# Score matmuls of 64 rows in the two halves of the array, and 256-column accumulators

## The chip, the cores and the metric

The kernel runs on one core of a Trainium2 chip. The metric is device time in microseconds (us) of one execution. The names of the engines are those of the profile: PE multiplies matrices (PEld is its weight load), DVE and ACT work element by element, POOL scatters rows, SP issues most DMAs. A matmul is written as 128x512 when it streams 512 columns through the array; its weights are loaded by an instruction of its own ahead of it.

## The reference

```python
scores = (1 / S) * z @ z.T               # z: 8 x 3072 x 64
attn = maximum(scores, 0) ** 2
x = (u * (attn @ v)).reshape(B * S, D)    # u, v: 8 x 3072 x 256
e = argmax(x @ w_gate)                    # 8 experts, in token order, 768 rows each at most
out = gate * (relu(disp[e] @ w1[e]) @ w2[e])   # F = 1024; rows past the capacity stay 0
```

Float32 products are made of fp16 pieces: each operand is split into a high and a low part (`h`, `l`), and a product is hi*hi + hi*lo + lo*hi, added up in float32 in PSUM. The gate decides which expert a row goes to, so the low parts cannot be left out.

## The kernel before

**Attention** goes by blocks of 512 queries (`CC` = 4 chunks of 128), 14 of them, the last a half block of 2 chunks; later tokens find all experts full. Six blocks are a batch. A block has 12 pairs of key tiles (`NPAIR`; a tile is 128 keys). For a pair the scores of two tiles are made (`scores`, L757 to L816), ACT takes the ReLU out of PSUM (L780) and squares both tiles at once (L784), DVE splits the squares into fp16 parts `hl` (L788, L797), and PE multiplies these with the split values `v2` (L872, L874) into the block's accumulators `acc`. Scores are symmetric, so a block whose mirror was computed earlier reads its scores back from DRAM, transposed by the DMA (`keep` L809, `load` L750, tile `ld`). 106 pairs are computed, 84 of them 512 columns wide and 22 of them 256 wide; the rest is loaded, or comes from a block's own corner (`corner`).

`zz` holds the split z, transposed, on 128 partitions: in `zz[:, 0]` the high part stands in partitions 0 to 63 and the low part in 64 to 127, in `zz[:, 1]` the other way round. So a tile's scores are two matmuls of all 128 rows (L772): one gives hi*hi + lo*lo, the other hi*lo + lo*hi.

A chunk's product with a key tile is two matmuls: the high weights against high and low values side by side, 512 columns (L872), and the low weights against the high values, 256 columns (L874). The accumulator has 512 columns, and its two halves are added when the block ends (`drain`, L839 on ACT, L840 on DVE). After that `route` multiplies with u (L556), finds the row's maximum (L561), splits, transposes, makes the gate's logits (`lg`), the running count (`cum`), and scatters the rows to their experts.

**Experts**: per expert up to 768 rows, `hps` (L1012, three matmuls per product as above) and `yps` (L1033, L1034, built like the attention's product), then ACT and DVE scale and add the two halves (L1040, L1043) and POOL scatters.

PSUM has 8 banks: 2 for scores (`sc`, and `yps`), 4 for accumulators (`acc`, and `hps`), 2 for the small tiles (`m`: transposed z, logits, counts).

The order of the work is written by a planner inside the kernel: it runs the instructions of PE in program order and keeps a clock per engine from a table of costs (`op`); pieces of work on the other engines wait in chains, and `weave` emits those that are due by these clocks. `need` marks what PE waits for. Scores are emitted up to three pairs ahead, one tile in each half of a pair. Costs are 0.864 us for 1024 columns of scores (L774) and 0.325 us for a chunk's product with a tile (L876).

## Time and profile before

| | us |
|---|---|
| median of 3 runs (lowest, highest) | 807.35 (807.35, 810.51) |
| the profiled execution | 808.55 |
| its span, first to last instruction | 806.7 |

| engine | busy, share of the span |
|---|---|
| PE | 781.0 us, 97% |
| DVE | 536.7 us, 67% |
| ACT | 434.3 us, 54% |
| POOL | 130.2 us, 16% |

The profile is one execution. Matmuls overlap in it: a record runs from a matmul's start until its last result, and the next one starts long before that. What a matmul costs PE is therefore the distance from its start to the next start, not the length of its record.

### The profile page before, as it was taken

How to read it: one execution, taken by the hardware profiler on the slowest of the kernel's cores; microseconds unless marked ns; L12 is line 12 of the kernel's file. 1: busy time of each engine (PE TensorE's matmuls, PEld its weight loads, DVE VectorE, ACT ScalarE, POOL GpSimd, SP SyncE). 2: the span in 40 equal slices, each digit the busy share in tenths (PEclk: the TensorE clock that was granted, in tenths of full speed). 3: DMA queues.
4: the chain of work that ended last, by engine and by line, in shares of the span. 5: the costliest groups of instructions: out<-in, count | busy, mean ns of one | idle time of the engine just before them, and what ended most of it. 6: DMA issues, size and time to landing. Idle time of an engine off the chain costs nothing.

```text
span 806.7 us, 13434 instructions
## 1 busy us (share of the span) xinstructions
PE 781.0 (97%) x4964; PEld 460.7 (57%) x4964; DVE 536.7 (67%) x1186; ACT 434.3 (54%) x748; POOL 130.2 (16%) x123
## 2 busy tenths in 40 slices
PE   6999999999999999999999999999799999999996
PEld 2555555555655555555556655565566666666663
DVE  6886887863536889976454359888674675665741
ACT  5786746461405767763524148674564564554541
POOL 0000121110202010202112020203211313303202
PEclk8799999999999999999999999999999999999999
DMA  6399998969897996949597969972797847655001
GB/s 195 131 339 253 309 256 205 262 173 226 187 202 154 305 281 168 277 129 269 136 270 172 202 153 297 272 188 78 183 323 291 260 137 285 217 164 173 27 14 44
DMA packets 278736, 165.48 MB, mean 205 GB/s; under 512 B 218125, under 2 KB 244058, under 8 KB 278656
## 3 DMA queue, kind: packets, MB, share of 16 engines
q1 hardware_dynamic: 273760, 151.69, 71.3%
q0 software_dynamic: 4896, 12.79, 4.7%
q8 instruction: 42, 0.69, 0.4%
q14 instruction: 38, 0.31, 0.1%
HBM read 35.86 MB, written 77.75 MB: 141 GB/s over the span
## 4 chain that ended last, share of the span: by engine, by line
PE 87%; DMA 5%; DVE 3%; SPq 2%; ACT 2%; issue 1%; POOL 0%; POOLq 0%; ACTq 0%
PE acc L872 32%; PE acc L874 16%; PE hps L1012 14%; PE sc L772 10%; PE yps L1033 10%; PE yps L1034 5%; DMA ld<-kept 2%; DMA vraw<-in_v 1%; DMA fxt<-disp 1%; DMA zz<-zhl 1%; SPq L584 1%; DVE hh L998 1%; PE lg L591 0%; SPq L343 0%; ACT r L780 0%
## 5 line engine op out<-in xcount | busy, mean ns | idle before, releaser
L872 PE MATMUL acc<-v,hl 128*128 128x512 f16 x760 | 257.7, 381 | 2.9 <-DVE v L459 2.9
L874 PE MATMUL acc<-v,hl 128*128 128x256 f16 x760 | 208.2, 274 | 0.0
L780 ACT ACTIVATE r<-sc 128x512 f32<-128x512 f32 (+1 forms) x212 | 116.1, 551 | 140.3 <-PE sc L772 133.4
L872 PE MATMUL acc<-v,ld 128*128 128x512 f16 x488 | 162.4, 379 | 3.4 <-DMA ld<-kept 2.0
L874 PE MATMUL acc<-v,ld 128*128 128x256 f16 x488 | 133.0, 272 | 0.0
L1012 PE MATMUL hps<-fxt,wt 128*128 128x384 f16 (+2 forms) x816 | 127.2, 316 | 4.0 <-DVE hh L998 1.8
L1033 PE MATMUL yps<-wt,hh 128*128 128x512 f16 x384 | 125.5, 379 | 0.0
L872 PEld LDWEIGHTS <-hl 128*128 128x128 f16 x760 | 74.7, 98 | 88.4 <-issue 1.9
L772 PE MATMUL sc<-zz 128*128 128x512 f16 (+1 forms) x424 | 118.6, 364 | 3.6 <-DVE zz L395 2.3
L797 DVE TENSOR_TENSOR hl<-a,hl 128x1024 f16<-128x1024 f32 (+1 forms) x106 | 118.2, 1115 | 3.5
L84 POOL DMA_INDIRECT disp<-xr,slot x54 | 67.6, 1252 | 300.0 <-ACT a L784 147.7
L1012 PEld LDWEIGHTS <-wt 128*128 128x128 f16 x816 | 76.0, 98 | 54.1 <-issue 5.1
L1034 PE MATMUL yps<-wt,hh 128*128 128x256 f16 x384 | 104.7, 273 | 0.4 <-DVE hh L998 0.4
L788 DVE CAST hl<-a 128x1024 f16<-128x1024 f32 (+1 forms) x106 | 67.9, 640 | 54.9 <-ACT a L784 47.7
L784 ACT ACTIVATE a<-r 128x1024 f32<-128x1024 f32 (+1 forms) x106 | 102.6, 968 | 3.2
L998 DVE SCALAR_TENSOR_TENSOR hh<-hps,hh 128x384 f16<-128x384 f32 (+2 forms) x136 | 70.7, 530 | 39.2 <-ACT hh L997 38.8
L997 ACT ACTIVATE hh<-hps 128x384 f16<-128x384 f32 (+2 forms) x136 | 62.9, 471 | 49.6 <-PE hps L1012 49.0
L874 PEld LDWEIGHTS <-hl 128*128 128x128 f16 x760 | 74.7, 98 | 24.2 <-issue 2.2
L872 PEld LDWEIGHTS <-ld 128*128 128x128 f16 x488 | 47.7, 98 | 56.9 <-DMA ld<-kept 3.3
L84 POOL DMA_INDIRECT out<-ys,sid x48 | 55.2, 1150 | 124.3 <-DVE ys L1043 86.1
L1033 PEld LDWEIGHTS <-hh 128*128 128x128 f16 x384 | 37.5, 98 | 44.1
L1040 ACT ACTIVATE ys<-yps,sg 128x256 f32<-128x256 f32 x48 | 22.8, 475 | 74.1 <-PE yps L1034 67.1
(134 smaller groups left out, 685.1 us busy)
## 6 DMA issues: line engine op xcount, KB each, us to landing
kept<-hl SPq DMA_DIRECT2D x62, 512.0 KB
out<-zero SPq DMA_DIRECT2D x48, 512.0 KB
wraw<-in_moe_w SPq DMA_DIRECT2D x32, 512.0 KB
vraw<-in_v SPq DMA_DIRECT2D x18, 512.0 KB
u<-in_u SPq DMA_DIRECT2D x13, 512.0 KB
disp<-dinit SPq DMA_DIRECT2D x8, 792.0 KB
zraw<-in_z SPq DMA_DIRECT2D x2, 768.0 KB
zz<-zz SPq DMA_DIRECT2D x4, 384.0 KB
```

What stands on the lines that cost most here:

```text
L84: r = nc.gpsimd.indirect_dma_start(out=dst, out_offset=bass.IndirectOffsetOnAxis(ap=idx, axis=0), in_=src, in_offset=None, bounds_check=bo ...
L772: nc.tensor.matmul(s[:, 0:w], lhsT=bt.zz[:, 0, j * P:(j + 1) * P], rhs=bt.zz[:, r, q0:q0 + w], start=(r == 0), stop=(r == 1))
L780: nc.scalar.activation(sct[p][:, jj, :], s[:, 0:w], AF.Relu)
L784: nc.scalar.activation(sq[p], sct.pop(p), AF.Square)
L788: nc.vector.tensor_copy(hl[:, :, :, 0, :], sq[p].rearrange("p j (t k) -> p j t k", k=HB))
L797: nc.vector.tensor_sub(hl[:, :, :, 1, :], a.rearrange("p j (t k) -> p j t k", k=HB), hl[:, :, :, 0, :])
L872: nc.tensor.matmul(o, lhsT=a(0, jj, c), rhs=bt.v2[:, j], start=(j == 0), stop=False, skip_group_check=True)
L874: nc.tensor.matmul(o[:, 0, :], lhsT=a(1, jj, c), rhs=bt.v2[:, j, 0, :], start=False, stop=(j == JT - 1), skip_group_check=True)
L998: [("DVE", 0.07 + w * 0.00104, lambda: nc.vector.scalar_tensor_tensor(out=tl, in0=src, scalar=0.0, in1=th, op0=ALU.max, op1=ALU.subtract), ...
L1012: nc.tensor.matmul(o, lhsT=wx.w1[:, d, wp, f * P:(f + 1) * P], rhs=sx.xt[:, xp * DC + d, a:a + w], start=(q == 0), stop=(q == len(seq) - 1))
L1033: nc.tensor.matmul(y, lhsT=hid(0, f)[:, sl], rhs=w, start=(f == 0), stop=False, skip_group_check=True)
L1034: nc.tensor.matmul(y[:, 0], lhsT=hid(1, f)[:, sl], rhs=w[:, 0], start=False, stop=(f == FC - 1), skip_group_check=True)
```

## The change

- **Scores.** Two computed pairs that follow each other form a team. A tile's three products are three matmuls of 64 rows, without lo*lo. One tile of a pair uses partitions 0 to 63 and the other 64 to 127, each with a PSUM bank of its own, and the two take turns. A team is 12 matmuls in a row and takes 4 banks of `sc`. It is emitted ahead of the third pair before its first one.
- **Products.** A chunk's product with a tile is three matmuls of 256 columns in one 256-column accumulator, two chunks to a bank. A block takes 2 banks; 3 are used in turn. `yps` is built the same way.
- **Drain.** One DVE instruction for two chunks multiplies the accumulator with u; the copy on ACT, the add on DVE and the product in `route` are gone. For `yps` the scaling on ACT remains and the add is gone.
- **PSUM.** `sc` (and `hps`) 4 banks, `acc` (and `yps`) 3, `m` 1. A flag `small` in the planner holds back the next small tile until the last one has been read. In SBUF `hl` goes from 4 to 5 buffers and `u` from 2 to 1.

```diff
-                st.tp = ps.tile([P, 2, 4, P], F16, tag="m", name="ztp")
+                st.tp = ps.tile([P, 2, 4, P], F16, tag="m", name="ztp", bufs=1)
...
-            s = ps.tile([P, BLK], F32, tag="sc", name="sc")
-            for r in range(2):
-                nc.tensor.matmul(s[:, 0:w], lhsT=bt.zz[:, 0, j * P:(j + 1) * P], rhs=bt.zz[:, r, q0:q0 + w],
-                                 start=(r == 0), stop=(r == 1))
-            t = op("PE", 0.864 * w / 1024, t)
...
+            for p in ps_:
+                if place[p] >= 2:
+                    t = max(t, need((aid, "r", place[p] - 2)))
...
+                s = [ps.tile([P, BLK], F32, tag="sc", name="sc", bufs=4) for _ in range(2)]
+                for i, (kl, ql) in enumerate(((0, 0), (0, 1), (1, 0))):
+                    for jj in (0, 1):
+                        rows, j = slice(DQ * jj, DQ * (jj + 1)), 2 * (p % NPAIR) + jj
+                        nc.tensor.matmul(s[jj][:, 0:w], lhsT=bt.zz[rows, (kl + jj) % 2, j * P:(j + 1) * P],
+                                         rhs=bt.zz[rows, (ql + jj) % 2, q0:q0 + w], start=(i == 0), stop=(i == 2))
+                t = op("PE", 0.1 + 3 * w / 2400, t)
+                follow(p, s, w, t)
...
-                hl = sb.tile([P, 2, nt, 2, HB], F16, tag="hl", name="hl", bufs=4)
+                hl = sb.tile([P, 2, nt, 2, HB], F16, tag="hl", name="hl", bufs=5)
...
-            o, x = acc[n][c], xs[n][:, c]
-            Chain([[("ACT", 0.35, lambda: nc.scalar.copy(x, o[:, 1]), None)],
-                   [("DVE", 0.34, lambda: nc.vector.tensor_add(x, x, o[:, 0]), (aid, "x", n, c))]],
-                  -2, clk["PE"])
+            o, x, w = acc[n][h], xs[n], ut[n]
+            sl = slice(2 * h, 2 * h + 2)
+            Chain([[("DVE", 0.65, lambda: nc.vector.tensor_mul(x[:, sl], o, w[:, sl]), (aid, "x", n, h))]],
+                  -2, max(clk["PE"], done["u", aid, n]))
...
+                    k = bank[0] - 3
+                    if k in held:
+                        clk["PE"] = max(clk["PE"], need((aid, "x", *held[k])) + HOP)
...
-                    nc.tensor.matmul(o, lhsT=a(0, jj, c), rhs=bt.v2[:, j], start=(j == 0), stop=False,
-                                     skip_group_check=True)
-                    nc.tensor.matmul(o[:, 0, :], lhsT=a(1, jj, c), rhs=bt.v2[:, j, 0, :], start=False,
-                                     stop=(j == JT - 1), skip_group_check=True)
-                    op("PE", 0.325, 0.0)
+                    for h, l in ((0, 0), (0, 1), (1, 0)):
+                        nc.tensor.matmul(o, lhsT=a(h, jj, c), rhs=bt.v2[:, j, l], start=(j + h + l + c % 2 == 0),
+                                         stop=(j == JT - 1 and h == 1), skip_group_check=True)
+                    op("PE", 0.328, 0.0)
...
-                nc.tensor.matmul(y, lhsT=hid(0, f)[:, sl], rhs=w, start=(f == 0), stop=False, skip_group_check=True)
-                nc.tensor.matmul(y[:, 0], lhsT=hid(1, f)[:, sl], rhs=w[:, 0], start=False, stop=(f == FC - 1),
-                                 skip_group_check=True)
+                for i, l in ((0, 0), (0, 1), (1, 0)):
+                    nc.tensor.matmul(y, lhsT=hid(i, f)[:, sl], rhs=w[:, l], start=(f + i + l == 0),
+                                     stop=(f == FC - 1 and i == 1))
```

How the instructions stand on PE in the first block, before: two matmuls of one tile's scores (`sc`, weights and columns out of `zz`), then the first product of a chunk (`acc`, weights `hl`, values `v2`).

```order
L772 LDWEIGHTS zz_122
L772 MATMUL sc_460<-zz_122 128x512
L772 LDWEIGHTS zz_122
L772 MATMUL sc_460<-zz_122 128x512
L872 LDWEIGHTS hl_428
L872 MATMUL acc_276<-v2_263,hl_428 128x512
```

Each tile has its two matmuls between two chunks' products, and PE goes straight on.

PE in the first block, after, where a team's first pair (`sc_427` and `sc_428`, a bank for each tile) gives way to its second (`sc_435` and `sc_436`).

```order
L787 LDWEIGHTS zz_122
L787 MATMUL sc_427<-zz_122 128x512
L787 LDWEIGHTS zz_122
L787 MATMUL sc_428<-zz_122 128x512
L787 LDWEIGHTS zz_122
L787 MATMUL sc_435<-zz_122 128x512
L787 LDWEIGHTS zz_122
L787 MATMUL sc_436<-zz_122 128x512
```

The matmuls of the two halves alternate, and four tiles stand in one piece where four places had one tile each.

The end of the same team, after, and the chunk's product behind it.

```order
L787 LDWEIGHTS zz_122
L787 MATMUL sc_436<-zz_122 128x512
L906 LDWEIGHTS hl_393
L906 MATMUL acc_293<-v2_279,hl_393 128x256
L906 LDWEIGHTS hl_393
L906 MATMUL acc_293<-v2_279,hl_393 128x256
```

Here PE goes over from weights of 64 rows to weights of 128 rows; at a team's start it goes the other way, and every product has one weight load more than before.

DVE at the end of the first block, before: the split of two pairs of the next block (`hl`), the four adds of the drain (`x<-x,acc`), the two products with u, the row maximum.

```order
L788 CAST hl<-a 128x4x256
L797 TENSOR_TENSOR hl<-a,hl 128x4x256
L840 TENSOR_TENSOR x<-x,acc 128x256 x4
L556 TENSOR_TENSOR x<-x,u 128x512 x2
L561 TENSOR_REDUCE rm<-x 128x4
```

The same place after.

```order
L862 TENSOR_TENSOR x<-acc,u 128x512
L812 CAST hl<-a 128x4x256
L821 TENSOR_TENSOR hl<-a,hl 128x4x256
L812 CAST hl<-a 128x2x256
L821 TENSOR_TENSOR hl<-a,hl 128x2x256
L862 TENSOR_TENSOR x<-acc,u 128x512
L572 TENSOR_REDUCE rm<-x 128x4
```

The six instructions of drain and product have become two, one for each bank, and the split of two pairs has moved in between them.

## Rows read from the trace of the kernel before

**Rows 1.** The page: busy time by engine, and the ending chain's shares.

```profile
PE 781.0 (97%) x4964; PEld 460.7 (57%) x4964; DVE 536.7 (67%) x1186; ACT 434.3 (54%) x748; POOL 130.2 (16%) x123
PE 87%; DMA 5%; DVE 3%; SPq 2%; ACT 2%; issue 1%; POOL 0%; POOLq 0%; ACTq 0%
```

**Rows 2.** Windows: stretch, length, busy us by engine (instructions), granted clock, DMA share, GB/s.

```profile
20.00:30.00 10.00, 8.27 (x35) 4.44 (x35) 9.05 (x27) 6.27 (x10) 1.70 (x2) 0.51 0.01 2
106.00:541.00 435.00, 429.16 (x2775) 254.10 (x2773) 293.32 (x655) 230.55 (x385) 56.96 (x48) 1.00 0.90 216
541.00:581.00 40.00, 35.59 (x290) 21.54 (x288) 30.37 (x110) 19.39 (x48) 11.79 (x12) 1.00 0.50 134
```

**Rows 3.** Timeline of PE: start us, length, instruction, its count; rows merge equal neighbours.

```profile
299.98 0.27 PE L874 MATMUL acc<-v,ld 128*128 128x256 f16 x1
300.09 0.38 PE L772 MATMUL sc<-zz 128*128 128x256 f16 x2
300.31 0.38 PE L872 MATMUL acc<-v,ld 128*128 128x512 f16 x1
...
303.13 0.59 PE L772 MATMUL sc<-zz 128*128 128x512 f16 x2
303.56 0.38 PE L872 MATMUL acc<-v,ld 128*128 128x512 f16 x1
...
304.86 0.59 PE L772 MATMUL sc<-zz 128*128 128x512 f16 x2
```

**Rows 4.** PE's groups of instructions: count, busy us, mean ns of one, idle before.

```profile
L772 PE MATMUL sc<-zz 128*128 128x512 f16 x336 | 101.8, 388 | 3.6 <-DVE zz L395 2.3 <-ACT r L780 1.3
L772 PE MATMUL sc<-zz 128*128 128x256 f16 x88 | 16.8, 273 | 0.0
L874 PE MATMUL acc<-v,hl 128*128 128x256 f16 x760 | 208.2, 274 | 0.0
L872 PEld LDWEIGHTS <-hl 128*128 128x128 f16 x760 | 74.7, 98 | 88.4 <-issue 1.9
L1033 PE MATMUL yps<-wt,hh 128*128 128x512 f16 x384 | 125.5, 379 | 0.0
```

**Rows 5.** Windows for line L872 alone, all shapes of weights: PE busy us (count).

```profile
0.00:807.00 807.00, 435.94 (x1296) 127.09 (x1296) 0.99 0.76 205
```

**Rows 6.** The ending chain in order of time, two experts' `hps`: start us, length.

```profile
612.35 15.60 PE hps L1012 x96
643.55 15.60 PE hps L1012 x96
```

**Rows 7.** ACT's and DVE's groups: count, busy us, mean ns of one, idle before.

```profile
L840 DVE TENSOR_TENSOR x<-x,acc 128x256 f32<-128x256 f32 x54 | 22.0, 419 | 28.5 <-ACT x L839 27.8 <-issue 0.4
L1043 DVE SCALAR_TENSOR_TENSOR ys<-yps,sg,ys 128x256 f32<-128x256 f32 x48 | 23.1, 481 | 54.3 <-ACT ys L1040 51.4 <-issue 2.3
L780 ACT ACTIVATE r<-sc 128x512 f32<-128x512 f32 x168 | 99.5, 595 | 128.0 <-PE sc L772 121.7 <-issue 1.1 <-ACT a L784 0.7
L784 ACT ACTIVATE a<-r 128x1024 f32<-128x1024 f32 x84 | 88.7, 1056 | 2.5
```

**Rows 8.** PE's waits: what waited for what, us in total, times, longest us.

```profile
PE acc L872 <- DMA ld<-kept: 2.0, 2, 1.0
PE acc L872 <- DVE x L840: 1.3, 1, 1.3
PE hps L1012 <- DVE ys L1043: 0.9, 1, 0.9
```

**Rows 9.** Timelines of PE and DVE in the start.

```profile
26.15 1.89 PE L772 MATMUL sc<-zz 128*128 128x512 f16 x4 [0.73 <-DVE zz L395]
...
25.37 1.57 DVE L395 COPY zz<-ztp 128x512 f16<-128x512 f16 x2 [0.18 <-ACT zz L395]
```

**Rows 10.** Timeline of the end: ACT's scaling, DVE's add.

```profile
799.59 0.47 ACT L1040 ACTIVATE ys<-yps,sg 128x256 f32<-128x256 f32 x1 [2.12 <-PE yps L1034]
800.10 0.48 DVE L1043 SCALAR_TENSOR_TENSOR ys<-yps,sg,ys 128x256 f32<-128x256 f32 x1 [2.12 <-ACT ys L1040]
```

More of the change, by code (lines that the diff above doesn't have):

```diff
@@ L177, in attention_moe_kernel, with free, f @@
     done = {}
+    small = [False]
+    def free(fn):
+        def f():
+            fn()
+            small[0] = False
+        return f
     HOP = 0.2
@@ L704, in b @@
             nc.vector.tensor_tensor(out=redo, in0=more, in1=short, op=ALU.max)
-        Chain([[("PE", 0.1, a, None)], [("DVE", 0.3, b, None)]], rank, after)
+        Chain([[("PE", 0.1, a, None, "small")], [("DVE", 0.3, free(b), None)]], rank, after)
     def check_early(n, after):
@@ L712, in a @@
             st.t = counts()
-        Chain([[("PE", 0.1, a, None)],
-               [("DVE", 0.2, lambda: ts(short, st.t[0:1, 0:1], float(n) - 0.5, ALU.is_lt), None)]], 0, after)
-    AHEAD = 3
+        Chain([[("PE", 0.1, a, None, "small")],
+               [("DVE", 0.2, free(lambda: ts(short, st.t[0:1, 0:1], float(n) - 0.5, ALU.is_lt)), None)]], 0, after)
     HB = BLK // 2
@@ L739, in cornered @@
             return n > 0 and cc == CC and g == 2 * ib + 1
-        computed = [2 * p + jj for p in range(NP) if not is_kept(p) for jj in (0, 1)]
-        place = {k: i for i, k in enumerate(computed)}
+        computed = [p for p in range(NP) if not is_kept(p)]
+        place = {p: i for i, p in enumerate(computed)}
+        teams = deque(tuple(computed[i:i + 2]) for i in range(0, len(computed), 2))
+        assert all(len(t) == 2 and t[1] == t[0] + 1 and t[0] % 2 == 0 for t in teams)
         loads = deque(p for p in range(NP) if is_kept(p))
-        ahead = [0]
         def load(p):
@@ L821, in scores @@
-            Chain(st, -1, t, gate=(aid, "s", k // 2 - 1) if k > 1 else None)
-        def scores_to(k):
-            while ahead[0] < len(computed) and computed[ahead[0]] < k:
-                scores(*divmod(computed[ahead[0]], 2))
-                ahead[0] += 1
+            st = [[("ACT", 0.05 + w * 0.00084, relu(0), None), ("ACT", 0.05 + w * 0.00084, relu(1), (aid, "r", k))],
+                  [("ACT", 0.09 + w * 0.00168, square, (aid, "s", k))],
+                  [("DVE", 0.07 + w * 0.00107, hi, None, bt.key("vs")), ("DVE", 0.29 + w * 0.0021, lo, (aid, "a", p))]]
@@ L828, in ld_u, with scores_to @@
+            if p + 1 < NP and cornered(p + 1):
+                st.append([turn(0), turn(1)])
+            if cc == CC and (ib, g // 2) in bt.kept:
+                st.append([("SP", 1.46, keep, None)])
+            Chain(st, -1, t, gate=(aid, "s", k - 1) if k else None)
+        def scores_to(p):
+            while teams and teams[0][0] <= p:
+                team(teams.popleft())
         def ld_u(n):
             bt, ib, c0, cc = blocks[n]
-            ut[n] = sb.tile([P, cc, D], F32, tag="u", name="u")
+            ut[n] = sb.tile([P, cc, D], F32, tag="u", name="u", bufs=1)
@@ L843, in attention, with start_route @@
+        def start_route(n, rid):
+            bt, _, _, cc = blocks[n]
+            keys = [(aid, "x", n, h) for h in range(cc // 2)]
+            watchers.append((lambda: all(k in done for k in keys), lambda: route(
+                xs.pop(n), bt, max(done[k] for k in keys), LAG if n < len(blocks) - 2 else 0.5, cc, rid)))
         loads_to(1)
-        scores_to(4)
+        scores_to(0)
         for p in range(NP):
```

128 lines of the change are left out of this document (60 added, 68 removed).

## Prediction

> **What bounds the kernel now.** The page comes first: PE is busy 97% of the span, and of the chain that ended last 87% is PE [rows 1]. A busy share proves little where records overlap, so the second view is the windows by stage: from 106 to 541 us, nearly all of the attention, PE misses only 435.00 - 429.16 = 5.8 us, at full clock (1.00, 2.4 GHz), while DVE is busy 293 and ACT 231 of 435 us [rows 2]. The attention is bound by the columns that PE streams. The third view, PE's timeline, shows what a column costs: two score matmuls of 512 columns start at 303.13 and the next work at 303.56, so 0.43 us for two; from there to 304.86 lie four chunk products of 768 columns, 1.30 us, 0.325 us each [rows 3]. In the experts a period is 643.55 - 612.35 = 31.20 us, half of it 96 matmuls in 15.60 us [rows 6]; PE streams there without a break as well. So the question is what the change does to PE's columns and to the gaps between them.
>
> **Scores: what is taken away.** Before, a 512-column pair is 4 matmuls, 0.86 us, a 256-column pair 0.44 (two of them take 300.31 - 300.09 = 0.22) [rows 3]. The 336 and 88 matmuls [rows 4] are 84 and 22 pairs. After, a pair is six matmuls of half the rows. If two halves stream beside each other, that is three steps: 0.648 and 0.327 us. Saved are 84 x 0.216 + 22 x 0.109 = 20.5 us. No row of this trace shows a matmul of 64 rows, so that they overlap is the first thing that I assume. Bounds: three steps (20.5 us gained) or six (61.5 us lost, below).
>
> **Scores: what is added.** 106 pairs are 53 teams, and at both ends of each PE changes between weights of 128 and of 64 rows, 106 changes. No row shows one. The lower bound is nothing: PE goes today from products to scores without a gap [rows 3]. For the upper bound, what a change could expose: a 256-column record lasts 274 ns while the next start comes after 109, so 165 ns pass until the last result is out, and a weight load lasts 98 ns [rows 4]; a change that waits for both costs 0.263 us, or 27.9 us in all. I take 0.10 us, about one weight load that is no longer hidden, 10.6 us in all. The planner's table says the same: 0.1 us a pair over the streaming time, two pairs and two changes to a team. I give that entry weight because its others agree with the trace: 0.864 for a pair and 0.325 for a product, as measured above [rows 3].
>
> The Trainium skill (TensorEngine Tiling (Array Packing), Key Properties) states that switching the tiling mode drains TensorE, which speaks against the change. In today's rows nothing drains, but nothing switches either, so no run here shows it yet. By that rule a change would cost at least those 165 ns and the sum would be -0.8 us (rival 1).
>
> **Products.** Columns stay at 768 per product, in three matmuls instead of two. The fixed part of a matmul: an expert's period has 96 x 384 + 48 x 768 = 73,728 columns, 30.72 us at 2.4 GHz, in 192 matmuls; the other 0.48 us is 2.5 ns each [rows 6]. There are 1296 products in the attention [rows 5] and 384 in the experts [rows 4], so 1680 x 2.5 ns = 4.2 us. The third weight load, 98 ns by its record [rows 4], hides: from 299.98 three 256-column matmuls, each with its own load, take 0.33 us, as long as today's product [rows 3]. Bounds 0 to 0.005 us per product, 0 to 8.4 us.
>
> **Drain.** ACT's copies and DVE's adds (54 x 419 ns) go, and 48 adds of 481 ns go in the experts [rows 7]. Nearly all of that lies beside PE and is worth nothing. What lies on the path: the one wait of 1.3 us for an add of the drain and 0.9 us for one of `yps` [rows 8]; DVE's work between the attention's last product and the last rows' scatter, in a stretch where PE misses 4.4 of 40 us [rows 2]; the last add, 0.48 us, which stands alone between ACT and the last scatter [rows 10]. I credit 0.5 for the end and 1.5 of the rest, 2.0 us. Behind a removed wait the next one is late (the transposes, scatters and loads of the last rows stay), so the credit may be nothing, or 4.
>
> **What is moved, and its cover.** Banks: a block's first bank must be drained when the next block's third chunk begins; that leaves PE two chunks of the old and two of the new, 8 products or 2.6 us, for one DVE instruction, which in the new order stands ahead of two pairs' splits. Nothing, up to 1 us per block where DVE is behind. ReLUs: a team hands ACT four tiles at once, 2 x (2 x 595 + 1056) = 4.5 us [rows 7]; its first pair is needed three pairs, 3 x 8 x 0.325 = 7.8 us, after the team began, so it is covered, and in the first block the next team comes after 16 products and 1.5 us, 6.7 us. SP: a team's two pairs are written back one behind the other, and loads queue behind; loads cost PE 2.0 us in all today [rows 8]. I take no change, 4 us either way. The single `m` bank: in the start the third group of transposes must wait until the second has left the bank; today both leave in one piece, 1.57 us from 25.37, and the scores start at 26.15 [rows 9]. That is 0 to 1 us, and as much again if the low clock (0.51 between 20 and 30 us [rows 2]) lasts longer. I take nothing.
>
> **The sum.** -20.5 + 4.2 + 10.6 - 2.0 = -7.7 us. Against the profiled execution's 808.55 us (span 806.7 and 1.85 around it) that is 800.9; the median of the runs lies 1.2 lower, 807.35, so I predict 799.7.
>
> **Rivals.**
> 1. *Changes drain PE.* At 165 ns each the 106 changes cost 17.5 us and the sum is -0.8: 806.5, no change. At 263 ns, results and weights, 27.9 us: +9.6, 817, slower. It decides from 20.5 - 4.2 + 2.0 = 18.3 us, 0.173 us a change. For: the two kinds of weights never meet today, and a record's tail of 165 ns is there to be exposed. Against: today the next matmul starts 165 ns before the last results are out [rows 4], so results on their way hold up nothing.
> 2. *Changes are free.* -18.3: 789. For: today PE passes from scores to products and back with no gap at all [rows 3].
> 3. *A half's weights cannot be loaded under that half's own matmul.* Each of 6 steps in 53 teams then pays one load, 98 ns: 31.2 us, 831; if only half of the load is exposed, 815. Against: at full height 256-column matmuls with own loads follow at 0.11 us [rows 3]. The Trainium skill (TensorE: Matmul & The Clock Gate, Part 3: Packing small matmuls) says that a load overlaps matmuls in flight only when its row group differs; the trace disagrees at full height.
> 4. *The halves don't stream beside each other.* Then the change doesn't do what it says: six steps, 61.5 us more than forecast, 861. They write different banks and read different partitions, which is against it.
> 5. *The DMA takes the gain.* Its share is 0.90 in the attention [rows 2]; if PE waits for loads as much as it gains, 806. Against: blocks that load most have few computed pairs, so PE comes sooner where loads are few.
>
> **How the numbers follow.** Chances: forecast (a change of 0.06 to 0.13 us; 796 to 803) 0.46; drained at about 165 ns 0.17; drained with load 0.10; free 0.12; half loads 0.08; no overlap 0.03; DMA 0.04. A measurement of this kernel tells 0.5%, about 4 us, from no change: 803.3 and 811.4 are the limits. Faster: 0.45 of the forecast and 0.12, 0.57. Same: 0.01 + 0.17 + 0.04, 0.22. Slower: 0.10 + 0.08 + 0.03, 0.21. The range runs from 788 (free) to 817 (drained with loads); beyond it stay no overlap, the worse half loads and the free case with the DMA's better luck, under 0.2. The forecast's own range is 796 to 803.
>
> **What would show it.** In PE's timeline: 12 score matmuls from first start to the next product's start in 1.3 us plus both changes (1.5 by the forecast, 1.6 to 1.8 drained, 1.9 with exposed loads, 2.6 without overlap), with the two halves starting almost together. The gap from the last 256-column product to a team's first start, less 0.109 us, is the price of a change. Three product matmuls should start 0.109 us apart; 0.15 would say that the third load isn't hidden. PE's waits in the attention should stay near 6 us, and none should name the `m` tiles or the drain after the start. If teams take 1.5 us and the time doesn't fall, the gain went into waits, and the DMA's loads are the first to look at.

## The result, and the profile of the changed kernel

The changed kernel takes 815.46 us (median of 16 runs; lowest 810.41), the kernel before 807.95 beside it (16 runs, one of them a stray of 1174.45 us that the median leaves aside). The ratio is 1.0089, 95% interval 1.0069 to 1.0109: slower by some 7 us, where 8 us less were forecast. The profiled execution took 813.75 us, its span is 812.0.

The page, and the windows (columns as in [rows 2]); the last row is of the kernel before, for the stretch that [rows 2] lack:

```profile
PE 777.7 (96%) x6856; PEld 608.0 (75%) x6856; DVE 496.0 (61%) x1084; ACT 404.3 (50%) x694; POOL 121.6 (15%) x123
```

```profile
20.00:30.00 10.00, 4.68 (x24) 2.66 (x25) 7.58 (x18) 3.99 (x6) 0.00 (x0) 0.51 0.00 1
30.00:40.00 10.00, 10.00 (x75) 6.43 (x72) 7.84 (x19) 8.04 (x12) 1.70 (x2) 0.81 0.44 172
106.00:541.00 435.00, 426.82 (x4059) 348.41 (x4058) 279.06 (x613) 205.44 (x340) 56.12 (x52) 1.00 0.93 219
```

```profile
30.00:40.00 10.00, 10.00 (x64) 5.73 (x62) 8.34 (x19) 9.09 (x15) 0.00 (x0) 1.00 0.63 248
```

DVE and ACT have 41 and 30 us less to do than in [rows 1], and the time did not fall by it. Between 20 and 30 us PE does 4.7 us of work instead of 8.3 [rows 2], and in the 10 us behind it the granted clock is 0.81 where it was 1.00. The low clock as such is not what the start lost, by an estimate from both traces: what PE's matmuls that began at the lower of its two levels (1.2 GHz) took beyond their full-speed time, at most as much again, is 5.5 us ahead of block 1 before and 3.8 us after. In the attention PE misses 435.00 - 426.82 = 8.2 us instead of 5.8.

PE's timeline at a team of 12 matmuls of 512 columns, and PE's group of these:

```profile
209.27 3.76 PE L906 MATMUL acc<-v,ld 128*128 128x256 f16 x33
212.96 1.47 PE L787 MATMUL sc<-zz 64*128 64x512 f16 x12
214.36 1.81 PE L906 MATMUL acc<-v,ld 128*128 128x256 f16 x15
```

```profile
L787 PE MATMUL sc<-zz 64*128 64x512 f16 x504 | 65.3, 390 | 4.7 <-DVE zz L410 4.7
```

The team takes 214.36 - 212.96 = 1.40 us from its first start to the next product's; that is the median of all 36 teams of this kind. In the trace its 12 half matmuls begin in pairs, the two of a pair within 0.004 us of each other and the pairs some 0.216 us apart, as far as one matmul of 512 columns at full height. Six pairs are 1.30 us; the other 0.10 us is the change back to weights of 128 rows. The change into the team: 33 product matmuls from 209.27 end their starts' row at 209.27 + 33 x 0.109 = 212.87, the team starts at 212.96, some 0.09 us (the median over the teams is 0.096). So the halves overlap fully, and a change costs what was forecast.

PE's waits (compare [rows 8]), and one line of the kernel before that [rows 8] lack:

```profile
PE lg L602 <- DMA xt<-xr: 5.4, 7, 1.9
PE sc L787 <- DVE zz L410: 4.7, 3, 1.6
PE acc L906 <- DMA ld<-kept: 3.3, 2, 1.9
...
PE hps L1045 <- PEq L1178: 2.3, 1, 2.3
...
PE ztp L404 <- DVE zz L410: 1.9, 1, 1.9
...
PE acc L906 <- DVE x L862: 1.0, 2, 0.6
```

```profile
PE lg L591 <- DMA xt<-xr: 1.6, 2, 1.1
```

Two kinds have grown: transposed z in the start (`zz`, 4.7 and 1.9 us, where [rows 4] have 2.3) and the logits' rows (`xt`, 5.4 us instead of 1.6).

**An account of PE's time.** Each matmul should take its columns / 2.4 GHz + 2.5 ns until the next start, at least the 25 ns by which the logits' matmuls of 16 columns follow each other (half of it in a team, and 0.095 us for a change); what a start is later than that is counted as a wait, low clock included. The 8 us of the span that this leaves out lie ahead of the first matmul and behind the last. Here it is for the two kernels and for all the runs below, from the profiled executions, beside the measured times (the ratio is to the kernel before on the same chip, with its 95% interval):

| kernel | median us | ratio | streaming | changes | waits to block 1 | blocks 1 to 13 | experts |
|---|---|---|---|---|---|---|---|
| before | 807.95 | | 769.2 | 0 | 16.1 | 7.3 | 5.6 |
| changed | 815.46 | 1.0089 (1.0069, 1.0109) | 752.9 | 10.1 | 21.7 | 13.5 | 5.9 |
| e1 | 819.9 | 1.0150 (1.0120, 1.0180) | 773.4 | 0 | 18.3 | 10.5 | 5.5 |
| e2 | 821.42 | 1.0151 (1.0114, 1.0188) | 773.4 | 0 | 13.9 | 20.7 | 6.2 |
| e3 | 814.7 | 1.0069 (1.0045, 1.0093) | 752.9 | 10.1 | 18.7 | 16.2 | 6.3 |
| e4 | 821.73 | 1.0173 (1.0145, 1.0202) | 752.9 | 19.9 | 21.6 | 10.1 | 6.0 |
| e5 | 815.05 | 1.0118 (1.0091, 1.0145) | 752.9 | 10.1 | 20.3 | 13.4 | 5.6 |
| e6 | 808.89 | 1.0024 (1.0006, 1.0042) | 769.2 | 0 | 17.0 | 6.0 | 5.7 |
| e7 | 814.16 | 1.0088 (1.0056, 1.0120) | 752.9 | 10.1 | 20.8 | 13.6 | 5.8 |
| e8 | 813.58 | 1.0100 (1.0074, 1.0126) | 773.4 | 0 | 13.7 | 10.7 | 4.4 |
| e9 | 816.81 | 1.0137 (1.0093, 1.0181) | 752.9 | 10.1 | 20.9 | 13.1 | 6.3 |
| e10 | 813.21 | 1.0071 (1.0046, 1.0095) | 752.9 | 10.1 | 18.3 | 16.9 | 5.9 |
| e11 | 819.23 | 1.0166 (1.0128, 1.0204) | 752.9 | 10.1 | 17.8 | 16.4 | 10.2 |
| e12 | 822.47 | 1.0194 (1.0170, 1.0218) | 752.9 | 10.1 | 17.0 | 18.3 | 11.1 |
| e13 | 818.41 | 1.0103 (1.0046, 1.0159) | 752.9 | 10.1 | 21.3 | 15.3 | 9.0 |
| e14 | 816.43 | 1.0101 (1.0046, 1.0156) | 752.9 | 10.1 | 18.1 | 17.6 | 6.3 |
| e15 | 808.66 | 0.9987 (0.9965, 1.0008) | 769.2 | 0 | 16.3 | 4.2 | 7.2 |
| e16 | 817.72 | 1.0107 (1.0072, 1.0143) | 752.9 | 10.1 | 21.4 | 16.2 | 5.6 |
| e17 | 823.51 | 1.0180 (1.0154, 1.0206) | 752.9 | 10.1 | 20.4 | 25.0 | 5.4 |
| e18 | 821.07 | 1.0160 (1.0137, 1.0182) | 752.9 | 10.1 | 16.5 | 25.1 | 5.4 |

Streaming and changes together: 763.0 against 769.2, 6.2 us gained. Waits: 41.1 against 29.0, 12.1 us lost, 5.6 of them ahead of block 1 and 6.2 in the attention behind it. The difference, 5.9 us, is that of the spans (5.3) but for 0.6 us behind the last matmul. By the medians the kernels are 7.5 us apart; the account is of one execution of each.

That is also its limit. Executions of the changed kernel differ by 9 us (810.41 to 819.78). In the profiles of the five kernels that have the same work ahead of block 1 (changed, e5, e9, e13, e16), block 1 begins 3.3 to 4.7 us behind the kernel before. So a difference of 1 or 2 us in one line of the table is not told from chance.

### The profile page after: what moved, and what is told of

Its sections match the earlier page's. It is cut to its first block, busy times and chain, and to the rows that moved or that the text cites. A ratio compares the mean times of both kernels' runs of the same rounds, so it can differ in the third digit from the quotient of the medians.

```text
span 812.0 us, 17040 instructions
## 1 busy us (share of the span) xinstructions
PE 777.7 (96%) x6856; PEld 608.0 (75%) x6856; DVE 496.0 (61%) x1084; ACT 404.3 (50%) x694; POOL 121.6 (15%) x123
## 5 line engine op out<-in xcount | busy, mean ns | idle before, releaser
L906 PE MATMUL acc<-v,hl 128*128 128x256 f16 x2280 | 261.8, 274 | 3.1 <-ACT v L474 2.7
L906 PEld LDWEIGHTS <-hl 128*128 128x128 f16 x2280 | 220.6, 98 | 38.3 <-issue 8.2
L906 PE MATMUL acc<-v,ld 128*128 128x256 f16 x1464 | 167.1, 273 | 4.4 <-DMA ld<-kept 3.3
L906 PEld LDWEIGHTS <-ld 128*128 128x128 f16 x1464 | 140.6, 98 | 26.7 <-issue 6.9
L1067 PE MATMUL yps<-wt,hh 128*128 128x256 f16 x1152 | 127.9, 273 | 0.0
L1067 PEld LDWEIGHTS <-hh 128*128 128x128 f16 x1152 | 112.6, 98 | 14.0
L787 PE MATMUL sc<-zz 64*128 64x512 f16 (+1 forms) x636 | 73.4, 365 | 4.7 <-DVE zz L410 4.7
L584 ACT ACTIVATE xr<-x,rsr 128x256 f16<-128x256 f32 x54 | 25.2, 502 | 72.9 <-DVE rsr L60 62.9
L787 PEld LDWEIGHTS <-zz 64*128 64x128 f16 x636 | 27.1, 95 | 38.8 <-issue 12.7
L974 DVE SCALAR_TENSOR_TENSOR wt<-wraw,w1r,wt 128x1024 f16<-128x1024 f32 (+1 forms) x18 | 20.4, 1164 | 12.8 <-ACT wt L970 12.8
```

The costliest lines, as they stand in the source:

```text
L584: return lambda: nc.scalar.activation(st.x16[:, c, 0:D], st.x[:, c, :], AF.Copy, scale=st.rs[:, c:c + 1])
L787: nc.tensor.matmul(s[jj][:, 0:w], lhsT=bt.zz[rows, (kl + jj) % 2, j * P:(j + 1) * P], rhs=bt.zz[rows, (ql + jj) % 2, q0:q0 + w], start=(i ...
L906: nc.tensor.matmul(o, lhsT=a(h, jj, c), rhs=bt.v2[:, j, l], start=(j + h + l + c % 2 == 0), stop=(j == JT - 1 and h == 1), skip_group_chec ...
L1067: nc.tensor.matmul(y, lhsT=hid(i, f)[:, sl], rhs=w[:, l], start=(f + i + l == 0), stop=(f == FC - 1 and i == 1))
```

## Experiments

### Is it the streaming? e1, e2, e4

**e1: the changed kernel, its scores in matmuls of 128 rows again**, still in teams of two pairs over four banks.

```diff
-                for i, (kl, ql) in enumerate(((0, 0), (0, 1), (1, 0))):
-                    for jj in (0, 1):
-                        rows, j = slice(DQ * jj, DQ * (jj + 1)), 2 * (p % NPAIR) + jj
-                        nc.tensor.matmul(s[jj][:, 0:w], lhsT=bt.zz[rows, (kl + jj) % 2, j * P:(j + 1) * P],
-                                         rhs=bt.zz[rows, (ql + jj) % 2, q0:q0 + w], start=(i == 0), stop=(i == 2))
-                t = op("PE", 0.1 + 3 * w / 2400, t)
+                for jj in (0, 1):
+                    j = 2 * (p % NPAIR) + jj
+                    for r in range(2):
+                        nc.tensor.matmul(s[jj][:, 0:w], lhsT=bt.zz[:, 0, j * P:(j + 1) * P],
+                                         rhs=bt.zz[:, r, q0:q0 + w], start=(r == 0), stop=(r == 1))
+                t = op("PE", 0.864 * w / 512, t)
```

> The changed kernel with teams of two pairs, but each tile's scores in two matmuls of all 128 rows as before the change. Theory A (the halves gained on PE what the trace shows, waits elsewhere ate it): a team of two 512-column pairs goes from 1.50 us with its two changes to 1.73, a mixed one loses 0.13, so 36 x 0.23 + 12 x 0.13 = 10 us more, about 825 us if the waits stay. Theory B (the halves gained nothing, their changes cost what they save): no change, 815.

Measured: 819.9, half-way between the two theories. The halves are worth 4 to 5 us in time (1.0150 against 1.0089). In the account they are worth 20.5 - 10.1 = 10.4 us; the other 6 are waits that the kernel with halves has and this one has not (41.1 against 34.3 us). Its timeline shows the full rows without any gap at either end of the team: 33 product matmuls from 206.55 to 210.15, then 8 matmuls in 1.72 us.

```profile
206.55 3.76 PE L906 MATMUL acc<-v,ld 128*128 128x256 f16 x33
210.15 1.89 PE L787 MATMUL sc<-zz 128*128 128x512 f16 x8
211.87 1.47 PE L906 MATMUL acc<-v,ld 128*128 128x256 f16 x12
```

**e4: one pair at a time**, twice as many changes.

```diff
-        teams = deque(tuple(computed[i:i + 2]) for i in range(0, len(computed), 2))
...
+        teams = deque((p,) for p in computed)
```

> The changed kernel with teams of one pair, so 212 changes between 128 and 64 rows instead of 106; all else the same. Theory A (a change costs the 0.1 us that the trace shows): 106 more changes, 10.6 us more, 826. Theory B (the gap beside a team is hidden elsewhere, because the time goes by waits for DMA): no change, 815.

Measured: 821.73, 6 us over the changed kernel, again between the two theories. Twice the changes are 10 us more by the account, and 3.5 us of waits are gone. A team of six half matmuls:

```profile
304.19 0.82 PE L786 MATMUL sc<-zz 64*128 64x512 f16 x6
304.94 1.26 PE L905 MATMUL acc<-v,hl 128*128 128x256 f16 x10
```

0.75 us, 3 x 0.216 + 0.10: the same price for a change. The Trainium skill (TensorEngine Tiling (Array Packing), Key Properties) states that changing the tiling mode drains TensorE. A change does cost here, but 0.10 us and not the 0.165 us by which a matmul's record outlasts the next start.

**e2: the kernel before with the new products and the new drain alone**, scores and their two banks as before.

```diff
...
-                    nc.tensor.matmul(o, lhsT=a(0, jj, c), rhs=bt.v2[:, j], start=(j == 0), stop=False,
-                                     skip_group_check=True)
-                    nc.tensor.matmul(o[:, 0, :], lhsT=a(1, jj, c), rhs=bt.v2[:, j, 0, :], start=False,
-                                     stop=(j == JT - 1), skip_group_check=True)
+                    for h, l in ((0, 0), (0, 1), (1, 0)):
+                        nc.tensor.matmul(o, lhsT=a(h, jj, c), rhs=bt.v2[:, j, l], start=(j + h + l + c % 2 == 0),
+                                         stop=(j == JT - 1 and h == 1), skip_group_check=True)
...
```

> The kernel before with the three 256-column products, the accumulator of 256 columns (4 banks in turn) and the drain in one DVE instruction, also for yps; scores and the two small banks as before. Theory A (products cost 2 ns each, the drain is no burden): 807.9 + 3.4 less up to 2 us of waits, 808 to 811. Theory B (the new drain or the third weight load is what slows the changed kernel): 813 or more.

Measured: 821.42, 13 us over the kernel before, of which 4.2 are streaming. The rest are waits of blocks 1 to 13, 20.7 us where the kernel before has 7.3: theory B's time. One of them, PE first, then what ACT did:

```profile
316.91 0.59 PE L764 MATMUL sc<-zz 128*128 128x512 f16 x2 [3.09 <-ACT r L772]
```

```profile
315.76 0.61 ACT L410 ACTIVATE zhl<-zraw,zb 128x384 f16<-128x384 f32 x1 [5.25 <-DMA zz<-zhl]
316.29 0.58 ACT L772 ACTIVATE r<-sc 128x512 f32<-128x512 f32 x1
```

```profile
318.00:320.00 2.00, 2.00 (x10) 1.29 (x9) 1.97 (x3) 1.97 (x3) 0.00 (x0) 0.50 0.66 130
```

ACT works in order. Its next instruction is the split of the next batch's z (`zhl`), which waits 5.25 us until an earlier piece has been transposed by a DMA and its buffer is free; behind it stands a ReLU, and PE waits 3.09 us for that one's bank. After this stop the granted clock is 0.50 for two us, 1.2 GHz instead of 2.4. The drain is one short step now, so that a block's row maximum, the route's first step behind the products with u, begins 0.77 us after the end of the block's last product (2.1 to 3.5 us in the kernel before) and the route falls into this work.

### The start: e3, e6, e7

In the start of the changed kernel PE, then DVE (compare [rows 9]):

```profile
26.61 1.01 PE L404 MATMUL ztp<-ident,zhl 128*128 128x128 f16 x8 [1.85 <-DVE zz L410]
29.20 2.32 PE L787 MATMUL sc<-zz 64*128 64x512 f16 x10 [1.58 <-DVE zz L410]
```

```profile
25.84 0.72 DVE L410 COPY zz<-ztp 128x512 f16<-128x512 f16 x1
28.42 0.72 DVE L410 COPY zz<-ztp 128x512 f16<-128x512 f16 x1 [1.86 <-ACT zz L410]
```

The scores that began at 26.15 now begin at 29.20. In the program the groups of z come out in another order than before: first, third, second. With four banks for scores, the planner reaches the first pair, which is the third group's gate, before the bits of v, which are the second group's. (e1, with four banks and full rows, has the same two waits here, 1.85 and 1.58 us; e6 below, with one `m` bank and two for scores, waits ahead of the transposes alone, 1.58 us.) The third group takes the one `m` bank, and the second, which these scores need, is copied out at 28.42 only.

**e6: the kernel before with one `m` bank** and the flag, order unchanged (one line of the edit; the flag's are left out).

```diff
-                st.tp = ps.tile([P, 2, 4, P], F16, tag="m", name="ztp")
+                st.tp = ps.tile([P, 2, 4, P], F16, tag="m", name="ztp", bufs=1)
```

> The kernel before, with nothing changed but the small results: z's transposed blocks, logits, running counts and counts share one bank of PSUM instead of two, with the same flag that keeps the planner from giving it out twice. Theory A, one bank is enough, as the prediction took it (0 to 1 us), and the start of the changed kernel is lost by the order in which it transposes the groups of z, not by the bank: 808 to 809, and block 1 begins within 1 us of the kernel before. Theory B, the single bank holds up the start and the routes: 811 to 814, with block 1 of the first batch 2 us or more later.

Measured: 808.89, and block 1 begins 0.9 us later than in the kernel before: theory A. The bank is not what costs the 4.7 us at block 1, but it is not free: the ratio, 1.0024 (1.0006 to 1.0042), stands for 0.5 to 3.4 us.

**e7: the changed kernel, z's groups in the `m` bank and an accumulator's bank in turn**, order unchanged (one line of the edit).

```diff
-                st.tp = ps.tile([P, 2, 4, P], F16, tag="m", name="ztp", bufs=1)
+                st.tp = ps.tile([P, 2, 4, P], F16, tag="m" if g % 2 else "acc2", name="ztp", bufs=1)
```

> The changed kernel, with z's groups transposed into the single small bank and into the third accumulator bank in turn, so that the third group no longer keeps the second from its bank (its order in the program stays: first, third, second). Theory A, the bank is what the second team of scores waits for at 28 to 29 us: the start of block 1 comes 3 to 4 us sooner than in the changed kernel and the time is 811 to 812. Theory B, it is the order (the second group's work stands behind the third's on every engine): block 1 less than 1.5 us sooner, 814 to 815.

Measured: 814.16; block 1 begins 0.95 us sooner than in the changed kernel, half of it gained ahead of block 0. That is within what kernels with the same start differ by. Theory B: it is not the bank.

**e3: the changed kernel with the groups in order.**

```diff
-                        Chain(z_group(g), -1, done[key("s")], gate=("pair", max(2 * g - 5, 0)) if g > 1 else key("vs"))
+                        Chain(z_group(g), -1, done[key("s")], gate=("pair", max(2 * g - 5, 0)) if g > 2
+                              else key("z", 1) if g > 1 else ("pair", 0))
```

> The changed kernel with one gate changed, so that the transposes of the second group of z take the one small bank before those of the third. Theory A (in the start the third group holds the bank, and the scores that need the second group wait about 2.6 us longer, at the low clock): 2.5 to 5 us less, 810 to 812.5. Theory B (the start is bound by the values' load and preparation, as before the change): no change, 815.

Measured: block 1 begins 3.0 us sooner than in the changed kernel (1.7 instead of 4.7 us behind the kernel before), so the order is what costs most of the start. The other kernels with z in order and the same work ahead of block 1 (e10, e11, e12, e14) bear this out: theirs begins 0 to 1.3 us behind the kernel before. But the time, for which theory A had 810 to 812.5, is 814.7, and the ratio's interval overlaps with the changed kernel's: in this profile the waits of blocks 1 to 13 are 16.2 us instead of 13.5. What the start gave back did not reach the end.

### The attention: e5, e8, e9, e15

**e5: logits put in 5.0 instead of 2.5 us after their rows are thought to be there.**

```diff
-    LAG = 2.5
+    LAG = 5.0
```

> The changed kernel with one number of the planner changed: it gives the router's transposed rows 5.0 instead of 2.5 us on their way before it puts the logits into TensorE's row (all blocks but the last two). Theory A, the logits are put in too early for the transfers of the now denser route, and TensorE, which stands in order, waits there: the seven waits of a logits matmul for the DMA of xt, 5.4 us in the profile of the changed kernel, go to under 2 us, and the time falls by 3 to 4 us, to 811 to 812.5. Theory B, the transfers themselves are late and the wait only moves to the next thing that needs the queue (half loads, the next batch's z, the flag of block 13): 815 as the changed kernel, with the same sum of waits in blocks 1 to 11 (10.9 us).

Measured: 815.05, and the waits of blocks 1 to 13 are 13.4 us as before: theory B. The waits for `xt` fell from 5.4 to 2.5 us, and a wait of 4.1 us for a loaded pair (`ld`) came in block 2.

**e8: e2 with the route begun 1.5 us later** by the planner's clock.

```diff
-                xs.pop(n), bt, max(done[k] for k in keys), LAG if n < len(blocks) - 2 else 0.5, cc, rid)))
+                xs.pop(n), bt, max(done[k] for k in keys) + 1.5, LAG if n < len(blocks) - 2 else 0.5, cc, rid)))
```

> The kernel with only the new products and drain (821.4, 13 us over the kernel before, 4.2 of them streaming), with one number changed: the planner lets a block's route begin 1.5 us later than its last drain, as late as it began in the kernel before (2.1 us and more after the block's last matmul, against 0.77). Theory A, the early start of the route is what costs the rest, because its work on VectorE and ScalarE then falls between that of the next batch's z and the scores: the waits of blocks 1 to 13 fall from 20.7 us to 10 or less, and the time to 810 to 813. Theory B, they come from the drain or the accumulators themselves: 820 to 822 again.

Measured: 813.58, 8 us less than e2, and waits of 10.7 instead of 20.7 us: nearly theory A, whose bounds were 813 and 10. The gain is less certain than the two medians say. e2 and e8 ran on different chips, and by their ratios to the kernel before it is 4 us, with intervals that overlap; the profiles are e2's slowest execution and e8's fastest. Nor did the whole route move: the row maximum still begins 0.8 us after the last product in nine blocks and came later, by 1.2 to 4.9 us, in blocks 5, 6, 11, 12 and 13 only. The stop shown above, behind block 6, is gone with that, and block 7's waits went from 4.9 to 0 us; so for that stop, as far as one profile of each shows, it is the early route that costs.

The profiled execution (812.46) is 3.9 us over that of the kernel before, and the waits in all are the same (28.9 and 29.0 us): in it the products cost their 4.2 us of streaming and no more. By the ratio (1.0100) e8 is 8 us over the kernel before, so what the other executions lose beyond the 4 us is open.

**e9: the same line in the changed kernel.**

> The changed kernel with the one number that took 8 us from the kernel with the products alone: the planner lets a block's route begin 1.5 us later than its last drain. Theory A, the early route is also what the attention of the changed kernel waits for: the waits of blocks 1 to 13 fall from 13.5 us towards the 7.3 of the kernel before, and the time falls by 4 to 6 us, to 809 to 811. Theory B, the changed kernel's waits come from its denser scores and from its start: under 2 us less, 813.5 or more.

Measured: 816.81. Theory A falls, and the time is theory B's. Here too the row maximum came later in blocks 5, 6, 11, 12 and 13 only (by 2.5 to 6.6 us). The waits of blocks 1 to 5 went from 8.0 to 4.6 us and those of blocks 12 and 13 from 2.6 to 0.2, but in block 7 a new one came, 6.1 us for one drain:

```profile
305.99 2.29 PE L906 MATMUL acc<-v,ld 128*128 128x256 f16 x10 [6.09 <-DVE x L862]
```

```profile
301.96 0.61 ACT L428 ACTIVATE zhl<-zraw,zb 128x384 f16<-128x384 f32 x1 [13.07 <-DMA zz<-zhl]
```

ACT stood 13 us for the transfer that frees a `zhl` buffer; DVE's half of that split waits for ACT, the drain stands behind it on DVE, and PE's second bank of block 7 waits for the drain.

**e15: the kernel before with its route 1.5 us later.**

```diff
-                route(xs.pop(n), ut.pop(n), bt, t,
+                route(xs.pop(n), ut.pop(n), bt, t + 1.5,
```

> The kernel before with the route of a block begun 1.5 us later in the planner, nothing else. Theory A, the kernel before waits little in the attention (7.3 us) because its order happens to fit, and any shift of its order brings waits of some us as in the changed kernel: 811 or more, waits of blocks 1 to 13 of 10 us or more. Theory B, its slack is real (two results less often ready than a denser row wants): within 2 us of 807.

Measured: 808.66, the same time, with 4.2 us of waits in the attention. Theory B: this shift, which delayed the row maximum in seven of the 14 blocks by 0.4 to 4.2 us, costs the kernel before nothing, so its few waits do not hang on that one number.

### What the waits hang on: e13, e14, e16, e17, e18

**e16, e13, e14: a fourth buffer for `zhl`** (its last group goes to the experts' input buffer, idle then): in the changed kernel (e16), in e9 (e13), and in e9 with the groups of z in order (e14).

```diff
-                st.zhl = sb.tile([P, ZW, 2, DQ], F16, tag="zhl", name="zhl", bufs=3)
+                if t0 + ZW < JT:
+                    st.zhl = sb.tile([P, ZW, 2, DQ], F16, tag="zhl", name="zhl", bufs=3)
+                else:
+                    st.zhl = sb.tile([P, ZW, 2, DQ], F16, tag="fxt", name="zhl")
```

> The changed kernel with the route 1.5 us later (816.8), and the last of the four groups of the second and third batch's z split into a buffer of its own (that of the experts' input, idle then), so that ScalarE no longer waits for the transfer of the first group. Theory A, the chain SyncE's queue, zhl, ScalarE, VectorE, drain is the 6.1 us wait of block 7: it goes, and the time is 810 to 812. Theory B, the drain waits for something else on VectorE, or the wait moves to the z that is then finished no sooner: 815 to 817.

> The same with z's groups in order in the start as well (813.2 without the fourth buffer). Theory A: 6 us less, 806 to 808, as fast as the kernel before, since the start gives 3 and the chain 6. Theory B: 812 to 814.

> The changed kernel with the fourth zhl buffer alone. In its trace ScalarE waits 7.9 us for that transfer at 293 to 301 us, but TensorE then only 0.6 us for the drain at 304. Theory A, the wait was nearly all hidden there: 0.5 to 1 us less, 814 to 815. Theory B, what is queued behind ScalarE in both batches (ReLU, the split) also costs the routes that follow: 2 us or more less, 811 to 813.

Measured: 818.41, 816.43 and 817.72. ACT's wait for that transfer is gone in all three, and in e13 and e14 the drain's wait of 6.1 us in block 7, as theory A said; but the time did not fall, and all three lie above what either theory had (e13 818.41 where B had 815 to 817). A few us further on in the same block PE waits for the corner's transposes instead (e13):

```profile
315.91 0.84 PE L909 MATMUL acc<-v,corner 128*128 128x256 f16 x6 [2.76 <-DMA corner<-hl]
```

So the splits wait no more, but PE waits for transposes instead. What these transfers share is SP's queue. SP in the changed kernel, at the turn from batch to batch, and then in the kernel before:

```profile
112.63 4.36 SPq L761 DMA_TRANSPOSE ld<-kept  x1
117.08 1.23 SPq L435 DMA_TRANSPOSE zz<-zhl  x1
118.41 2.83 SPq L761 DMA_TRANSPOSE ld<-kept  x1
121.33 1.24 SPq L435 DMA_TRANSPOSE zz<-zhl  x1
...
124.40 1.98 SPq L435 DMA_TRANSPOSE zz<-zhl  x1
126.48 2.80 SPq L827 DMA_TRANSPOSE corner<-hl  x2
129.46 2.50 SPq L595 DMA_TRANSPOSE xt<-xr  x2
132.06 1.24 SPq L435 DMA_TRANSPOSE zz<-zhl  x1
133.39 3.13 SPq L595 DMA_TRANSPOSE xt<-xr  x2
```

```profile
102.94 1.46 SPq L417 DMA_TRANSPOSE zz<-zhl  x1
...
108.06 1.46 SPq L417 DMA_TRANSPOSE zz<-zhl  x1
...
116.53 1.23 SPq L417 DMA_TRANSPOSE zz<-zhl  x1
...
118.49 1.22 SPq L417 DMA_TRANSPOSE zz<-zhl  x1
119.88 5.20 SPq L584 DMA_TRANSPOSE xt<-xr  x4
```

Each transpose takes SP over 1.2 us to issue, one behind the other. Before, the next batch's four stand ahead of the router's rows. In the changed kernel they come 8 to 14 us later (block 2 begins 2 us later) and among them: the load of that z was issued 5.7 us after block 1 began, where it was issued 2.6 us ahead of it. But the turn is nearly full in both kernels. The windows there, the changed kernel and then the one before:

```profile
100.00:140.00 40.00, 35.79 (x333) 28.62 (x333) 31.75 (x65) 17.74 (x30) 5.11 (x6) 1.00 1.04 244
```

```profile
100.00:140.00 40.00, 36.70 (x233) 20.99 (x232) 31.75 (x66) 21.65 (x36) 6.86 (x7) 1.00 1.02 235
```

The DMA share is 1.04 and 1.02, and SP's DMA instructions last 37.2 and 34.6 of the 40 us (from 106 to 541 us 338 and 329 of 435).

**e17: the next batch prepared four pairs (11 us) earlier; e18: that, with z in order.**

```diff
-            if g == 0 and ib == (b == 0) and b + 1 in bats:
-                prepare(bats[b + 1])
+            n2, g2 = divmod(p + 4, NPAIR)
+            b2, ib2 = divmod(n2, BPB)
+            if g2 == 0 and ib2 == (b2 == 0) and b2 + 1 in bats:
+                prepare(bats[b2 + 1])
```

> The changed kernel with one edit: the preparation of the next batch is begun four pairs of key tiles (some 11 us) before the block at which it began. Theory A, the late load of the next batch's z is what makes its transposes meet those of the corner and the router's rows on SyncE's queue: the waits of blocks 2 and 3 (0.6, 2.0, 0.9, 1.2, 1.6 and 0.9 us, 7.3 in all) go to under 3 us, the sum of blocks 1 to 13 from 13.5 to about 9, and the time to 809 to 811. Theory B, the transfers are too dense there in whatever order: the waits appear at other steps of blocks 1 to 4, the time stays at 814 to 817.

> The same with the groups of z in order in the start (3 us less at block 1). Theory A: both gains add up, 806 to 808, the kernel before's time. Theory B: 812 to 815, as with the order alone (814.7).

Measured: 823.51 and 821.07, slower than either theory had. In blocks 2 and 3 theory A held: in the account their six waits, 7.3 us, became two, 0.4 and 1.5 us. But in block 1 of e17 a single wait took 12 us. PE, then SP:

```profile
93.22 0.27 PE L602 MATMUL lg<-wg,xt 128*128 128x16 f16 x4 [12.13 <-DMA xt<-xr]
```

```profile
73.69 3.45 SPq L827 DMA_TRANSPOSE corner<-hl  x2
77.19 2.98 SPq L355 DMA_DIRECT2D vraw<-in_v  x4
80.22 1.80 SPq L301 DMA_DIRECT2D disp<-dinit  x3
82.13 10.44 SPq L595 DMA_TRANSPOSE xt<-xr  x4
```

Block 0's logits stood in PE's row from 81 us on. Their rows were ready at 80.1, but their transposes stood behind the loads of v, which had come forward with z, and behind the first writes of `disp`, and took 2.6 us each on average (the median of such a transpose is 1.2 us in the kernel before). What left one place of the queue came back at another.

### Two more settings: e10, e11, e12

e10 is e9 with the groups of z in order, e11 that with `LAG` at 3.5 (block 12 too), e12 that with the route 3.0 us later and `LAG` at 2.5 for block 12 too.

> Late route and the groups of z in order, together. If the two losses are separate, the start gives back 3 us (block 1 begins 1.7 instead of 4.7 us later than in the kernel before) and the late route what it gives alone: 3 us under the kernel with the late route alone, 806 to 808. If what the start gains is always taken back at the next batch's z (as in the kernel with z in order alone, where block 13 began 2 us later again), it equals the late route alone.

> As the kernel with late route and z in order, and the logits put in at 3.5 instead of 2.5 us, those of block 12 too (0.5 before). If the waits of logits for xt (7 of them, 5.4 us in the changed kernel, 2.0 of it in block 13) are the last loss, 2 to 3 us under the kernel without this number, 804 to 806; if they only move to the half loads, as the later logits alone did (a wait of 4.1 us for a half load came in block 2), the same time.

> Z in order, the route 3.0 us later instead of 1.5, and block 12's logits at 2.5 us. If what matters is that the route doesn't begin before the scores that follow the block are through their first steps, 3.0 does as 1.5 does, within 2 us; if each us of delay moves waits on to the end of the route (xt lands later, the logits wait), it is 3 us or more slower than 1.5.

Measured: 813.21, 819.23 and 822.47; e10 lies between its two expectations, e11 above both, e12 is 9 us over e10, the worse of its two cases. By their ratios e10 and e3 are the fastest of the kernels with halves, 0.7% slower than the kernel before; with z in order the late route gives nothing. e11 and e12 were no better in the attention and 4 to 5 us worse in the experts (10.2 and 11.1 us of waits). No kernel here beats the one before; e15, that kernel with a later route, equals it.

## Why the prediction was wrong

1. **What bounds the kernel: right for the kernel before, and not enough for the changed one.** PE misses only 5.8 of 435 us there. The forecast counted PE's columns well: streaming and changes fell by 6.2 us, where -20.5 + 4.2 + 10.6 = -5.7 was forecast.
2. **Halves beside each other, and the price of a change: right.** A pair of half matmuls takes 0.216 us. A change costs 0.10 us, as forecast. Rivals 1 to 4 fall: a drain as in rival 1 would make a team with both its changes 1.63 us and more (1.30 and 2 x 0.165), free changes 1.30, half loads 1.9, no overlap 2.6, where 1.40 and the 0.10 ahead of it were measured, 1.50 in all. (The prediction expected both changes between a team's first start and the next product; one lies ahead of the first start.) That rivals 1 and 3 named times of 817 and 815 is chance: their mechanisms do not occur. One bound was mislabelled: 61.5 us for no overlap is the distance from the forecast; against the kernel before it would be 41 us.
3. **Products: right.** Three per product start 0.109 us apart, so the third load hides, and the 4.2 us are in the account. In time the price alone is less well shown: e8 is 3.9 us over the kernel before in the profile, 8 us by its ratio.
4. **Drain, credit of 2.0 us: wrong in its larger part.** Behind the last matmul 0.6 us went (0.5 was credited). The 1.5 us for the waits ahead did not come: the experts' waits are 5.9 us against 5.6. And a faster drain is no gain where nobody waits for it: in e2 it let the route begin among the splits of the next batch's z.
5. **"I take no change, 4 us either way" and "I take nothing" for the waits: these two steps failed.** Waits grew by 12.1 us. In the start I priced the one `m` bank at 0 to 1 us, and e6 bears that out, 0.9 us at block 1 in its profile. I missed that four banks for scores change the order in which the planner lets the groups of z through; that order costs 3.0 of the 4.7 us by which block 1 is late (e3). In the attention I looked at each wait for itself and found its cover. I did not ask what the planner's new order does to SP's queue as a whole. The prediction's last sign held in the main: teams take 1.5 us with their changes, the time did not fall, and the gain went into waits. But the loads named as the first suspect hold little of it (`ld` 3.3 us against 2.0); `xt` holds more (5.4 against 1.6).
6. **Rival 5, the DMA takes the gain, had 0.04 and was the nearest in kind.** Its price was not: 806 (a gain fully lost to waits would be 807) allowed for no loss beyond the gain. My argument against it was that blocks which load most have few computed pairs. Most of the attention's waits are elsewhere: at the turns between batches, where loaded pairs, corner, router's rows and the next batch's z and v share SP's queue. The DMA share, 0.90 in the attention, should have warned: for the 8 us of the forecast the same transfers would have had to fit into less time.

What is shown: the streaming, the start's order, and that in the attention waits of this kernel can be taken away one by one (for `xt` in e5, for `zhl` and the drain in e13, in blocks 2 and 3 in e17) while their sum stays between 13 and 25 us (10 in e4, whose changes cost PE 10 us more); the kernel before takes one shift of its route without loss (e15). The cause of the 6.2 us that the attention lost stays open. What is argued only: that the queue is too full at those turns for any order. The kernel before has a DMA share of 1.02 at the turn too, so fullness alone does not tell the two apart. No run here made the transfers fewer, so an order that would keep the 6 us of streaming is not excluded.

## What to carry to other kernels

A gain in the engine that bounds a kernel is a gain only if the waits do not grow by as much. Where the DMA share is 0.9 already and one queue issues them in order, price the whole queue at its fullest stretch, not each wait. Where a planner sets the order, any change of buffers is also a change of order: compare the orders at the start and at each turn before calling a move free. And a wait that goes should be followed to the next one: take the sum of all waits of a stage, as in the account above, since single lines of the wait list went by 3 to 6 us here (5.4 to 2.5 in e5, 6.1 to none in e13) without the sum falling.

## What the hardware showed that was not expected

- Two matmuls of 64 rows in the two halves begin within 0.004 us of each other and take 0.216 us together for 512 columns each. A change between weights of 128 and 64 rows costs 0.10 us each way (1.40 us for a team of 12, 0.75 for one of six), less than the 165 ns by which a matmul's record outlasts the next start.
- A stop of PE of 3.1 us in full attention was followed by two us at a granted clock of 0.96, two at 0.50 and two at 0.69 (e2); that wait cost more than its length.
- A DMA transpose of the router's rows takes SP 1.2 us to issue in the kernel before (median of 54), and four took 2.6 us each on average just behind loads of v and writes of `disp` (e17).
